# Moving a fused attention and gated-MLP kernel's loads into one GpSimd queue, with cast on load and single-head transposes

## The chip, the cores and the metric

The kernel runs on one core of one Trainium2 chip. The metric is the device time of one execution in microseconds (us), as the median over several executions. A profile is a trace of one execution; its span is 1 to 2 us shorter than the device time. Engines are written as the profile writes them: PE is TensorE, PEld its weight loads, DVE VectorE, ACT ScalarE, POOL GpSimd, SP SyncE (here it only issues DMAs). A queue is the list of transfers that one engine issues, in its order; the core's 16 DMA engines move the data. A packet is one piece of a transfer as the trace records it. PSUM is the memory that the matmuls here write to.

## The reference, cut to what matters

Four batches; 8 heads of 64; 768 positions. A query sees 4 sink positions and a window of 128. The attention output x, 768 x 512 per batch, goes through a gated MLP whose gate mixes positions.

```python
scores = scale * np.matmul(q, k.transpose(0, 1, 3, 2))
keep = (pos[None, :] < n_sink) | in_window          # 4 sinks, window of 128
a = softmax(np.where(keep, scores, -1e9))
x = np.matmul(a, v)                                 # [4, 768, 8*64]
h = gelu(x @ w_in);  u, v = h[..., :512], h[..., 512:]
v_n = layernorm(v) * g_ln
v_s = np.einsum('ts,bsd->btd', w_sg, v_n) + b_sg
out = x + (u * v_s) @ w_out
```

## The kernel before

Both kernels are one list of steps, `STEPS`, that fixes the order of instructions on each engine. A step is a helper's name with batch and pair (or half): `LQ.3.0` loads q of batch 3, `TQ` and `EQ` turn it on TensorE and copy it out of PSUM, `AV` and `NR` make x, `MV` is the v half of the first projection, `RS` the LayerNorm's reciprocal root, `SP`, `GT`, `GM` the gate, `OU`, `RA`, `ST` the output projection, residual and store. Steps of neighbouring batches are interleaved.

All q, k and v loads went in one queue, SP's, in float32, and GpSimd cast each:

```python
def LQ(b, p):
    return nc.sync.dma_start(out=q32.new((b, p)), in_=q[b, 2 * p:2 * p + 2].rearrange("h (p t) d -> p h (t d)", p=128))
def LV(b, p):
    return nc.sync.dma_start(out=v32.new((b, p)).rearrange("p h t d -> p (h t) d"),
                             in_=v[b, 2 * p:2 * p + 2].rearrange("h (t p) d -> p (h t) d", p=128))
def CQ(b, p):     # CK, CV alike
    return cast(q16.new((b, p)).rearrange("p t h d -> p h t d"), ...)      # nc.gpsimd.tensor_scalar
```

For batches 1 to 3, x is turned by two DMA transposes, `XD`, issued on SP's queue too:

```python
def XD(b, half):
    ts = slice(3 * half, 3 * half + 3)
    return nc.sync.dma_start_transpose(out=xT.get(b)[:, ts, :, :].rearrange("p t c i -> p (t c) i"),
                                       in_=x_sb[b][:, ts, :].rearrange("p t d -> p (t d)"))
```

And their place in the order (cut to the loads, transposes and stores of that time): before, all of these are in one queue, so loads that stand behind a transpose cannot pass it.

```
... LQ.3.0 ... LK.3.0 ... XD.1.1 ... XD.1.0 ... ST.0.0 ... ST.0.2 ... LV.3.0 ... LQ.3.1 ... LK.3.1 ... ST.0.1 LV.3.1 ... LQ.3.2 ...
```

The softmax here doesn't subtract the row's maximum and nothing guards it: scores larger than these inputs give would overflow.

## Time and profile before

| | before |
|---|---|
| device time, median | 173.03 us (172.1 to 174.0, 4 runs) |
| span of the profile | 171.1 us |
| PE, DVE, ACT, POOL busy | 88%, 81%, 60%, 56% |
| first matmul of the first projection (MV of batch 0) | 33.5 us |
| DMA transposes, issue to landing | 3.7 to 5.0 us |

The page of the kernel before: busy share of each engine in tenths, in 40 equal slices of the span (4.28 us each), and the DMA queues (packets, MB, share of the time of 16 DMA engines).

```profile
PE   0447889699989899979999999999999999999970
...
DMA  5999989999999999989999200970100374210044
...
q1 hardware_dynamic: 47072, 27.93, 61.5%
q0 software_dynamic: 2368, 2.75, 9.8%
```

PE is nearly full from slice 19 on (counted from 1; 77 us); the losses are at the start. The DMA engines are nearly full up to slice 22. q1 is the queue that SP and ACT issue on; q0 is GpSimd's, which carried only the weights.

### The profile page before, as it was taken

What the parts mean: (1) busy time and instruction counts of PE and PEld (TensorE: products, weight loads), DVE (VectorE), ACT (ScalarE), POOL (GpSimd) and SP (SyncE); (2) the same over time, 40 slices, a digit from 0 to 9 for tenths busy, and PEclk for the clock granted to TensorE, in tenths of its full rate; (3) what the DMA queues carried; (4) which work ended last, traced back from release to release, by engine and by line L of the source; (5) the groups of instructions that cost most, each with busy time, mean ns of one, the idle gap of its engine ahead of it and who ended that gap; (6) DMA issues with size and microseconds to landing.
All of it is one profiled execution on the core that took longest, in us unless ns stands there. A gap on an engine that the chain in (4) does not pass through costs nothing.

```text
span 171.1 us, 3623 instructions
## 1 busy us (share of the span) xinstructions
PE 151.1 (88%) x1388; PEld 90.3 (53%) x1388; DVE 138.7 (81%) x290; ACT 101.9 (60%) x119; POOL 95.9 (56%) x158
## 2 busy tenths in 40 slices
PE   0447889699989899979999999999999999999970
PEld 0323568364655466645576565544565744556530
DVE  6198696629989999999999799848889994959962
ACT  0416887674995768956649985864997006860000
POOL 7789766013899999999599678043306400520000
PEclk9999999999999999999999999999999999999999
DMA  5999989999999999989999200970100374210044
GB/s 166 325 314 240 210 117 195 221 252 246 316 299 297 279 288 298 314 160 214 321 323 281 64 4 17 230 248 0 61 4 0 64 170 180 80 61 0 34 156 184
DMA packets 49617, 30.94 MB, mean 181 GB/s; under 512 B 35904, under 2 KB 46400, under 8 KB 49600
## 3 DMA queue, kind: packets, MB, share of 16 engines
q1 hardware_dynamic: 47072, 27.93, 61.5%
q0 software_dynamic: 2368, 2.75, 9.8%
q8 instruction: 11, 0.18, 0.4%
q10 hardware_dynamic: 160, 0.03, 0.1%
q14 instruction: 6, 0.05, 0.1%
HBM read 24.81 MB, written 6.29 MB: 182 GB/s over the span
## 4 chain that ended last, share of the span: by engine, by line
PE 63%; DVE 20%; ACT 5%; DMA 5%; POOL 3%; issue 2%; DVEq 0%; ACTq 0%
PE mm L466 15%; PE mm L483 11%; PE sc L446 10%; PE sc L399 10%; PE sc L310 5%; PE mm L266 4%; ACT P L318 3%; DVE qT L276 3%; DVE gtmp L471 3%; PE mm L350 3%; DVE x_sb L370 3%; DMA q<-in_q_dram 3%; DVE P L325 3%; DVE wsg_gated L476 2%; PE mm L356 2%
## 5 line engine op out<-in xcount | busy, mean ns | idle before, releaser
L318 ACT ACTIVATE P<-sc 128x1024 bf16<-128x1024 f32 (+1 forms) x48 | 43.7, 953 | 12.2 <-PE sc L310 10.6
L466 PE MATMUL mm<-wsgT,z 128*128 128x384 bf16 x192 | 34.0, 326 | 0.0
L329 POOL TENSOR_SCALAR_AFFINE_SELECT P<-P 128x512 bf16<-128x512 bf16 x28 | 20.1, 719 | 18.2 <-ACT P L318 13.8
L466 PEld LDWEIGHTS <-z 128*128 128x128 bf16 x192 | 18.0, 98 | 12.1 <-issue 1.2
L483 PE MATMUL mm<-w_out_sb,wsg_gated 128*128 128x512 bf16 x96 | 23.0, 379 | 1.1 <-DVE wsg_gated L476 1.1
L399 PE MATMUL sc<-w_in_sb,xT 128*128 128x512 bf16 x96 | 22.4, 379 | 0.2 <-ACT xT L384 0.2
L446 PE MATMUL sc<-xT,w_in_sb 128*128 128x384 bf16 x128 | 22.4, 326 | 0.0
L471 DVE SCALAR_TENSOR_TENSOR gtmp<-mm,g_sb,b_bc 128x384 bf16<-128x384 f32 x32 | 19.3, 611 | 3.6 <-PE mm L466 3.5
L487 DVE TENSOR_TENSOR ot<-mm,x_sb 128x512 f32<-128x512 f32 x24 | 16.1, 683 | 5.4 <-PE mm L483 5.3
L310 PE MATMUL sc<-qT,kT 64*128 64x256 bf16 x192 | 17.0, 287 | 3.8 <-DVE qT L276 1.7
L350 PE MATMUL mm<-v_sb,P 128*128 128x65 bf16 x192 | 18.0, 201 | 1.6 <-DVE P L325 1.4
L404 ACT ACTIVATE vt<-sc 128x1024 f32<-128x1024 f32 x12 | 12.3, 1024 | 11.7 <-PE sc L399 11.7
L182 POOL TENSOR_SCALAR q<-q 128x768 bf16<-128x768 f32 x16 | 14.3, 891 | 8.6 <-DMA q<-in_q_dram 8.6
L370 DVE TENSOR_TENSOR x_sb<-mm,rcp 128x384 bf16<-128x384 f32 x32 | 17.8, 557 | 1.1
L350 PEld LDWEIGHTS <-P 128*128 128x128 bf16 x192 | 15.2, 102 | 5.9 <-issue 2.1
L411 DVE BATCH_NORM_STATS2 st<-vt 128x6 f32<-128x512 f32 x24 | 16.2, 675 | 2.5 <-ACT vt L404 2.5
L325 DVE TENSOR_TENSOR P<-P,mask 128x1024 bf16<-128x1024 bf16 x20 | 16.4, 830 | 1.3 <-ACT P L318 1.1
L356 PE MATMUL mm<-v_sb,P 128*128 128x65 bf16 x160 | 16.9, 200 | 0.0
L446 PEld LDWEIGHTS <-w_in_sb 128*128 128x128 bf16 x128 | 12.4, 98 | 8.4
L281 ACT COPY kT<-mm 128x768 bf16<-128x768 bf16 x16 | 12.8, 801 | 5.6 <-PE mm L266 5.6
L182 POOL TENSOR_SCALAR v_sb<-v 128x768 bf16<-128x768 f32 x16 | 14.9, 937 | 1.9 <-DMA v<-in_v_dram 1.9
L418 POOL TENSOR_SCALAR rs<-mv 128x2 f32<-128x2 f32 x12 | 3.0, 251 | 22.6 <-DVE mv L412 22.2
(61 smaller groups left out, 253.8 us busy)
## 6 DMA issues: line engine op xcount, KB each, us to landing
q<-in_q_dram SPq DMA_DIRECT2D x16, 384.0 KB, 6.6
k<-in_k_dram SPq DMA_DIRECT2D x16, 384.0 KB, 5.8
v<-in_v_dram SPq DMA_DIRECT2D x16, 384.0 KB, 6.9
out_dram<-ot SPq DMA_DIRECT2D x24, 256.0 KB, 2.0
wsg_gated<-in_moe_w_sg_dram POOLq DMA_DIRECT2D x1, 1152.0 KB, 8.8
w_in_sb<-in_moe_w_in_dram POOLq DMA_DIRECT2D x2, 512.0 KB, 7.2
w_out_sb<-in_moe_w_out_dram POOLq DMA_DIRECT2D x1, 512.0 KB, 8.1
b_bc<-in_moe_b_sg_dram SPq DMA_DIRECT2D x1, 384.0 KB
```

What stands on the lines that cost most here:

```text
L182: return nc.gpsimd.tensor_scalar(out=dst, in0=src, scalar1=1.0, scalar2=1.0, op0=ALU.mult, op1=ALU.mult)
L310: nc.tensor.matmul(sc[:, hl, 256 * jl:256 * jl + n], kT[b, p][rows, 128 * j:128 * (j + 1)], qT[b, p][rows, 128 * j:128 * j + n], start=Tru ...
L318: nc.scalar.activation(out=pt[:, :, 0:w], in_=sc_ring[b, p, g][:, :, 0:w], func=AF.Exp, scale=scale)
L325: nc.vector.tensor_mul(pt[:, :, 0:w], pt[:, :, 0:w], m.unsqueeze(1).to_broadcast([128, 2, w]))
L350: nc.tensor.matmul(av[:, il, hl, :], P[b, p, i // 2][:, hl, 256 * (i % 2):256 * (i % 2) + 128], vb[:, h, i, :], start=first, stop=False)
L356: nc.tensor.matmul(av[:, il, hl, :], P[b, p, j // 2][:, hl, 256 * (j % 2) + 128:256 * (j % 2) + 256], vb[:, h, j, :], start=False, stop=False)
L370: nc.vector.tensor_mul(xs[:, 3 * half:3 * half + 3, 128 * p:128 * (p + 1)].rearrange("p t (h d) -> p t h d", h=2), av[:, :, :, 0:Dh], rcp. ...
L399: nc.tensor.matmul(hp[:, jl, :], xT[b][:, j, c, :], w_in_sb[:, c, d_half:2 * d_half], start=(c == 0), stop=(c == KD - 1))
L446: nc.tensor.matmul(hp[:, hf, 0:NH], w_in_sb[:, c, 128 * dc:128 * (dc + 1)], xT[b][:, 3 * hf:3 * hf + 3, c, :], start=(c == 0), stop=(c == ...
L466: nc.tensor.matmul(ps[:, 0:NH], z[b][:, si, 128 * dc:128 * (dc + 1)], wsgT[:, si, NH * hf:NH * (hf + 1)], start=(si == 0), stop=(si == NT ...
L471: nc.vector.scalar_tensor_tensor(out=gtmp.new((b, hf, dc)), in0=mm_ring["g", b, hf, dc][:, 0:NH], scalar=g_sb[:, dc:dc + 1], in1=b_bc[:, N ...
L483: nc.tensor.matmul(ps, gatedT[:, (2 * b + hf) % 3, dc, 128 * tl:128 * (tl + 1)], w_out_sb[:, dc, :], start=(dc == 0), stop=(dc == KU - 1))
```

## The change

The intent: free GpSimd of 42 of its 48 casts by letting the DMA cast q and k, for which they go to GpSimd's queue, and giving most of v's casts to DVE and ACT; keep all loads in one queue in the order in which they are needed, and use the freed time for masks and gating products that DVE did. q and k now lie head by head, so each 128 x 64 block of one head is turned alone, two heads side by side on the two column halves of the array. The sink scores of four head pairs also go side by side. The order of steps is new throughout. The diff, cut to its core (the new `STEPS`, the new places of masks, fills, LayerNorm scalars and gating products are left out):

```diff
-    def LQ(b, p):
-        return nc.sync.dma_start(out=q32.new((b, p)), in_=q[b, 2 * p:2 * p + 2].rearrange("h (p t) d -> p h (t d)", p=128))
+    def load(ring, src, b, i):
+        n = 2 if b == 0 else 4
+        hs = slice(n * i, n * i + n)
+        dst = ring.get((b, n * i // 4))[:, n * i % 4:n * i % 4 + n].rearrange("p h t d -> p h (t d)")
+        return nc.gpsimd.dma_start(out=dst, in_=src[b, hs].rearrange("h (p t) d -> p h (t d)", p=128))
...
     def LV(b, p):
-        return nc.sync.dma_start(out=v32.new((b, p)).rearrange("p h t d -> p (h t) d"),
-                                 in_=v[b, 2 * p:2 * p + 2].rearrange("h (t p) d -> p (h t) d", p=128))
+        return rows(nc.sync if b in DT else nc.gpsimd, v32, v, b, p)      # DT is empty
...
         for t in range(NT):
-            nc.tensor.transpose(ps[:, t, :], src[:, t, :], iden)
+            for hl in range(2):
+                nc.tensor.transpose(ps[64 * hl:64 * hl + 64, t, :], src[:, 2 * (p % 2) + hl, t, :], iden)
...
-        for n, p in enumerate(prs):
-            nc.tensor.matmul(ps, ks_sink[b % 2][:, 128 * p:128 * (p + 1)], qT[b, p][:, 256:768],
-                             start=(n == 0), stop=(n == len(prs) - 1))
+        for p in range(HP):
+            c0 = (128 + ks_w) * p
+            nc.tensor.matmul(ps[ks_w * p:ks_w * (p + 1), :], ks[:, c0:c0 + ks_w], qT[b, p][:, 256:768],
+                             start=True, stop=True)
```

In the new order batch 3's loads stand beside batch 1's transposes (again cut to the loads, transposes and stores). They are in different queues now:

```
... LQ.3.0 ... XD.1.0 ... LK.3.0 ... LV.3.0 ... LV.3.1 ... ST.0.1 ... XD.1.1 ... LQ.3.1 ... LK.3.1 ... LV.3.2 ... ST.0.3 MV.1.0 ... LV.3.3
```

## The prediction

> **What bounds the kernel now.** TensorE, behind a slow start. The page gives PE 88% busy, DVE 81%, ACT 60%, POOL 56%. "Busy" contains matmul latency, so I counted starts in the trace: back to back, a 512-column matmul follows after 216 ns, 384 columns after 162, a 128-column transpose after 56, 65 columns after 29, and two 64-row matmuls start 3 ns apart. At these cadences the PE streams about 135 us of 171. Of the 36 lost, about 23 lie before 35 us (first MV at 34.5 us in the chain of work that ended last), 4 to 5 in the tail, most of the rest at 45 to 75 us, where that chain runs through POOL (LayerNorm queued with casts, 41.2 to 47.6 us) and then DVE (50 to 74 us). From 80 to 160 us the PE streams 97% of the time.
>
> **What the change removes, adds, moves** (mean durations from the instruction groups)
> - POOL: 42 casts of 0.9 us go (-38), 7 affine-select pairs (-9), small LayerNorm operations (-5). It gains 34 load issues, 0.8 to 0.9 us each by the present weight loads (+31, more if 1,536-row v loads cost more), and 17 gating products (estimate 0.9 us, +16). Still near 90 us, but loads, masks and gating now wait behind each other.
> - DVE: 17 gating products (0.48 us) and 3 PSUM copies (0.95) go, -11; seven casts, seven masks, LayerNorm scalars and two xT copies come, about +11.
> - ACT: +4.
> - PE: sink scores of batches 1 to 3 go from four 216 ns matmuls to four side by side: -2 us. Transposes: 192 become 384 of half width. If two run together as the 64-row matmuls do, nothing changes; if their weight loads serialise, up to 0.3 us for each of 32 tiles, +10. The Trainium skill (TensorEngine Tiling, Restrictions) says column tiling excludes fast weight load; no trace here shows it yet. I take +3.
> - DMA: cast loads need the GpSimd queue (Trainium skill, DMA: Bandwidth & Descriptors, "SWDGE vs HWDGE vs iDMA"; the four weight loads agree). In the DMA records a packet of that queue costs about 13 ns more than one of the SP queue (98 against 85 ns at 2 KB, 22 against 9 at 4 B). So v rows go from 18 to about 31 ns, a v load from 1.8 to 3 us of all 16 engines. Total about 128 us: fits, but one ordered queue delivers batch 1's second q, k about 55 us, close to need.
>
> **On the critical path.** First scores (10.6 us now, held by DVE waiting for the sink v until 8.6 us) come 1 us earlier; first MV perhaps 2 to 3 earlier. LayerNorm/DVE stretch: -4 to -5. Sink scores -2, transposes +3, late batch-1 loads and port contention +1 to +2. Sum about -5.
>
> **Predicted: 168 us, 160 to 177 in 8 of 10. Faster by over 2%: 0.60; within 2%: 0.27; slower: 0.13.**
>
> **What would show it.** Right: first scores before 10 us; the GpSimd queue carrying nearly all load packets, 256 B ones near 31 ns; transposes in pairs a few ns apart, 12 in 0.35 to 0.45 us; no POOL cast of q or k after batch 0; PE idle of 45 to 75 us halved. Wrong: transposes at 50 ns each (+8); v issues above 1.5 us on POOL; PE waiting on DMA for batch 1's q or k; DVE waiting on POOL for gating.
>
> **What would make it wrong.** 256 B packets far above 31 ns; serial half-width weight loads; POOL blocked by a load whose buffer is not free, delaying masks.

## More of the kernel before

The instructions that read or write xT, the turned x, in the kernel before: count, duration in ns as least, median and most, first and last start; then who waited for it. The last line is from issue to landing.

```profile
L388 SPq DMA_TRANSPOSE xT<-x_sb x6: 1426/1452/1906, 71.5 to 137.6; - x6
...
DMA to landing us min/median/max: 3.7/4.3/5.0
```

SP's queue in the kernel before around batch 1's two transposes (start, duration of the issue in us, line, transfer). They stand at 71.46 and 76.28 us, and what follows them in the queue (the v loads from 79.23 on) starts after them.

```profile
71.46 1.91 SPq L388 DMA_TRANSPOSE xT<-x_sb  x1
74.72 0.34 SPq L490 DMA_DIRECT2D out_dram<-ot  x1
76.28 1.45 SPq L388 DMA_TRANSPOSE xT<-x_sb  x1
77.82 1.30 SPq L490 DMA_DIRECT2D out_dram<-ot  x2
79.23 0.39 SPq L178 DMA_DIRECT2D v<-in_v_dram  x1
```

## The result, and the profile after

The changed kernel took 184.19 us (183.81 to 185.47, 4 runs) against 173.03. The ratio of the two is 1.066, with a 95% interval of 1.058 to 1.074. (Every ratio here is the mean time of one kernel's fast runs over that of the other's of the same rounds, so it is not quite the ratio of the medians.) It is slower, and outside the predicted range of 160 to 177.

The same rows of the page after. A slice is now 4.6 us.

```profile
PE   0567948999799999459049999999999999999990
...
PEclk9996596999999999978858999999999999999999
DMA  5999999999995139999971000099000048111044
...
q0 software_dynamic: 12128, 14.94, 44.5%
q1 hardware_dynamic: 14240, 9.87, 21.0%
```

The hole is in slices 17 to 21 (73.5 to 96.5 us): PE reads 4, 5, 9, 0, 4 tenths, while the DMA row reads 9 there (7 in the last slice), so the engines that move data were busy while TensorE stood still. The granted clock drops in and after the hole: from 75 to 100 us PE was busy 13.0 of 25 us and its granted clock was 0.80 (in e1 below, without the hole, 23.8 us and 1.00). The chain of work that ended last, around the hole (start, duration, what):

```profile
71.53 0.54 PE sc L344 x8
72.07 1.06 PE mm L505 x5
73.14 21.32 DMA xT<-x_sb
94.46 0.05 issue
94.51 4.24 PE sc L428 x12
```

The chain hangs for 21.32 us on one transfer, batch 1's second transpose. The instructions on xT, and the longest waits of the kernel after on DMAs (engine, line, what it waited for: us in total, times, longest):

```profile
L419 SPq DMA_TRANSPOSE xT<-x_sb x6: 1323/1441/7436, 68.5 to 150.3; - x6
...
DMA to landing us min/median/max: 3.6/4.3/11.6
```

```profile
DVE ot L509 <- DMA out_dram<-ot: 13.4, 2, 7.4
PEld L428 <- DMA xT<-x_sb: 12.9, 2, 7.8
PE sc L428 <- DMA xT<-x_sb: 11.9, 2, 7.3
```

The median landing is as before, 4.3 us; one of six, batch 1's first, took 11.6, and by the chain the second took 21.3. (The line of landings covers only the transposes that the tool could match.) The stores of batch 0 on the same queue came late too. SP's queue at that time, and GpSimd's loads beside it (a line with x4 runs from the first issue to the end of the last, waits between them included):

```profile
68.47 2.08 SPq L419 DMA_TRANSPOSE xT<-x_sb  x1
72.41 0.34 SPq L512 DMA_DIRECT2D out_dram<-ot  x1
73.14 7.44 SPq L419 DMA_TRANSPOSE xT<-x_sb  x1
80.67 15.40 SPq L512 DMA_DIRECT2D out_dram<-ot  x4
```

```profile
67.92 0.80 POOL L182 DMA_DIRECT2D q<-in_q_dram  x1
68.71 0.90 POOL L182 DMA_DIRECT2D k<-in_k_dram  x1
69.60 1.04 POOL L185 DMA_DIRECT2D v<-in_v_dram  x1
...
71.81 1.07 POOL L185 DMA_DIRECT2D v<-in_v_dram  x1
```

Seven of batch 3's eight loads were issued from 67.9 to 75 us (the eighth at 76.8), on the other queue, in the same 10 us as the two transposes. They were not needed so soon: in the kernel before, all but two of batch 3's twelve (smaller) loads came after the transposes in the queue, from 79.23 us on.

What the DMA engines did then can be counted in the trace's DMA records: packets started in each 2 us, by queue and size. A transpose is 1,536 packets of 256 B; q and k travel as 768 B (the size written), v on GpSimd's queue as 4,096 B.

```
after            GpSimd 768 B   GpSimd 4096 B   SP 256 B (transposes)
72 to 74 us               151               0                     707
74 to 76 us               224               0                     695
82 to 84 us               258              11                     265
84 to 86 us               370               0                     384
86 to 88 us               275              34                     322
88 to 90 us                18              71                     104
90 to 92 us                 0              67                     143

the same transposes with the loads held back (experiment e1)
72 to 74 us               166               0                    1347
74 to 76 us                 0               0                    1270
```

From 82 to 88 us, where both queues had work throughout, the engines served about one packet of each in turn, with three times the bytes written for the loads; against v's 4,096 B the transposes got one to two packets per large one, and only 104 and 143 in 2 us. The first transpose, from 72 to 76 us, got three to five packets for each one of 768 B; why the shares differed there stays open. In e1, nearly alone, each transpose's 1,536 packets were through in 1.9 us, about 800 per us. The Trainium skill states such turns ("DMA: Bandwidth & Descriptors", section "Queues, rings and completion order"): each DMA engine goes round robin between the queues it has work for, packet by packet. The trace agrees with one turn each from 82 to 88 us, with 258:265 and 370:384, but not from 72 to 76 us, with 151:707 and 224:695.

The packets also divide the 21.32 us. For the first 5.3 us (73.1 to 78.5) the second transpose had no packet under way: in SP's own queue the first transpose (packets from 72.3 to 77.9 us) and a store (76.9 to 81.5) stood in front of it, both slowed. Its own packets then took 15.4 us, to 93.8; in e1 they took 1.9.

Before, the v loads that follow the transposes stood behind them in the same queue, and could not take turns with them.

### The profile page after: what moved, and what is told of

The parts are those of the page before. It is cut to its first block, busy times and chain, and to the rows that moved or that the text cites. A ratio compares the mean times of both kernels' runs of the same rounds, so it can differ in the third digit from the quotient of the medians.

```text
span 183.8 us, 3933 instructions
## 1 busy us (share of the span) xinstructions
PE 151.8 (83%) x1567; PEld 90.3 (49%) x1580; DVE 138.1 (75%) x307; ACT 105.3 (57%) x125; POOL 89.1 (48%) x121
## 2 busy tenths in 40 slices
DMA packets 26386, 25.06 MB, mean 136 GB/s; under 512 B 11136, under 2 KB 21632, under 8 KB 26368
## 3 DMA queue, kind: packets, MB, share of 16 engines
q0 software_dynamic: 12128, 14.94, 44.5%
## 4 chain that ended last, share of the span: by engine, by line
PE 68%; DMA 15%; DVE 7%; ACT 4%; issue 2%; SPq 1%; POOL 1%; DVEq 0%
PE mm L488 18%; DMA xT<-x_sb 12%; PE sc L468 11%; PE sc L428 10%; PE mm L505 10%; PE sc L344 6%; PE mm L294 4%; PE mm L384 4%; ACT P L352 3%; DMA vs<-in_v_dram 3%; PE mm L390 2%; PE mm L394 2%; DVE P L359 2%; DVE x_sb L404 1%; DVE v_sink L283 1%
## 5 line engine op out<-in xcount | busy, mean ns | idle before, releaser
L428 PE MATMUL sc<-w_in_sb,xT 128*128 128x512 bf16 x94 | 25.2, 419 | 12.2 <-DMA xT<-x_sb 11.9
L509 DVE TENSOR_TENSOR ot<-mm,x_sb 128x512 f32<-128x512 f32 x24 | 16.1, 686 | 19.8 <-DMA out_dram<-ot 13.4
L498 POOL TENSOR_TENSOR wsg_gated<-gtmp,uT 128x384 bf16<-128x384 bf16 x17 | 16.8, 991 | 18.7 <-DVE gtmp L493 18.4
L449 POOL TENSOR_TENSOR rs<-rs,neg_half 128x4 f32<-128x4 f32 (+1 forms) x8 | 6.9, 865 | 33.6 <-DVE rs L444 31.5
L505 PE MATMUL mm<-w_out_sb,wsg_gated 128*128 128x512 bf16 x87 | 22.3, 379 | 0.7 <-issue 0.3
L428 PEld LDWEIGHTS <-xT 128*128 128x128 bf16 x96 | 9.8, 106 | 25.4 <-DMA xT<-x_sb 12.9
L363 POOL TENSOR_SCALAR_AFFINE_SELECT P<-P 128x512 bf16<-128x512 bf16 x21 | 14.5, 689 | 15.6 <-ACT P L352 15.6
L359 DVE TENSOR_TENSOR P<-P,mask 128x1024 bf16<-128x1024 bf16 (+1 forms) x27 | 21.5, 816 | 0.0
L185 POOL DMA_DIRECT2D v<-in_v_dram x16 | 16.9, 1058 | 8.9 <-DMA wsg_gated<-in_moe_w_sg_dram 3.8
## 6 DMA issues: line engine op xcount, KB each, us to landing
k<-in_k_dram POOLq DMA_DIRECT2D x6, 384.0 KB, 15.4
```

The source lines that it names most:

```text
L185: return eng.dma_start(out=ring.new((b, p)).rearrange("p h t d -> p (h t) d"), in_=src[b, 2 * p:2 * p + 2].rearrange("h (t p) d -> p (h t) ...
L359: nc.vector.tensor_mul(pt[:, :, 0:w], pt[:, :, 0:w], m.unsqueeze(1).to_broadcast([128, 2, w]))
L428: nc.tensor.matmul(hp[:, jl, :], xT[b][:, j, c, :], w_in_sb[:, c, d_half:2 * d_half], start=(c == 0), stop=(c == KD - 1))
L505: nc.tensor.matmul(ps, gatedT[:, (2 * b + hf) % 3, dc, 128 * tl:128 * (tl + 1)], w_out_sb[:, dc, :], start=(dc == 0), stop=(dc == KU - 1))
```

## The experiments

All experiments edit the changed kernel's steps or one helper. Each was timed beside the kernel before on the same chip. The theory (A in the expectations) is that batch 3's loads on GpSimd's queue starve batch 1's transposes on SP's queue. Rivals: B, that the loads cost by themselves and not through the transposes (by their place in GpSimd's order of instructions, or v's loads by their issue and descriptors), or that dearer work on PE and DVE does; C, that the transpose stands behind a late store in SP's own queue.

### e1: hold batch 3's loads until the transposes have landed

```diff
-EX.1.3.2 TK.2.2 LQ.3.0 GT.0.1.2 XD.1.0 ... LK.3.0 ... LV.3.0 ... LV.3.1 ... XD.1.1 ... LQ.3.1 ... LK.3.1 ... LV.3.2 ... LV.3.3
+EX.1.3.2 TK.2.2 LQ.3.0 GT.0.1.2 XD.1.0 ... XD.1.1 ... MK.2.1.1.P LK.3.0 LV.3.0 LV.3.1 LQ.3.1 LK.3.1 LV.3.2 LV.3.3
-HOLDS = "LG<LWS"
+HOLDS = "LG<LWS LK.3.0<XD.1.1"
```

> The changed kernel with one move: the seven loads of batch 3 behind its first q load are issued after the masks that now follow them, and wait until batch 1's second DMA transpose has landed. Theory A (the DMA transposes of batch 1, made of 256 B packets on the SP queue, share each DMA engine turn by turn with the long packets of the GpSimd queue's loads): both transposes land within 5 us of issue, the 11.9 us of PE waiting for xT and most of the 13.4 us of DVE waiting for the output stores go, time 166 to 171 us. Theory B (the loads' place in the GpSimd instruction queue, or dearer PE and DVE work all over, makes the kernel slow): at most 4 us better, 180 to 184 us.

Measured: correct, 172.03 us (170.6 to 172.72), ratio to the kernel before 0.994 (0.987 to 1.002). The edit of seven loads' place gives back 12 us of 184.2. The transposes now land like this, and PE's wait for them and DVE's for the stores are gone from the list of waits:

```profile
L419 SPq DMA_TRANSPOSE xT<-x_sb x6: 1322/1440/1584, 68.6 to 136.6; - x6
...
DMA to landing us min/median/max: 3.7/4.3/6.3
```

That is theory A's main claim; and as PE and DVE have the same work as in the changed kernel, dearer work there is not the loss. Batch 1's first transpose took the 6.3 us, over the 5 that I expected (why is not shown); the second took 3.9, by its semaphore. And the time is 1 us over the range that I expected. The chain of e1 (start, duration, what) shows a new wait that the hold itself made:

```profile
77.71 0.80 POOL k L182
78.51 7.46 DMA v<-in_v_dram
85.97 0.08 issue
86.06 0.83 POOL v_sb L210
86.89 1.03 POOL rs L449
```

GpSimd waits until 85.97 us for a v load of batch 3 that is now late, to cast it, and only then computes `rs`, the LayerNorm of batch 1, for which DVE and TensorE wait. Experiment e5 follows this up.

### e2: turn batch 1's x on TensorE, loads where the change put them

```diff
-... XD.1.0 ... XD.1.1 ...
+... XT.1.0 XE.1.0.A XT.1.1 XE.1.1.D XT.1.2 XE.1.2.A XT.1.3 XE.1.3.D ...
```

> The changed kernel with batch 1's x turned by 24 TensorE transposes and four PSUM copies (two ACT, two DVE) instead of the two DMA transposes; the loads stay where they are. Theory A: the wait goes as well, since no small packets are on the critical path; PE pays about 1.4 us and the output stores still stand against the loads, so 167 to 173 us. Theory B: 181 to 186 us.

Measured: 171.38 us (170.54 to 171.84), ratio 0.990 (0.983 to 0.997), but the result was wrong (relative error 0.17): by my reading of the order, my insertion needed more PSUM slots than the ring of four has, so two steps read slots that had been overwritten. The time is as theory A expects, yet I did not lean on it; e7 is the same idea in an order that is right.

### e3: the store of batch 0 behind the transpose

```diff
-QK.2.0.1 ST.0.1 OU.0.5 EX.2.0.0 MK.2.0.2.D XD.1.1 KS.2.0
+QK.2.0.1 OU.0.5 EX.2.0.0 MK.2.0.2.D XD.1.1 ST.0.1 KS.2.0
```

> The changed kernel with the output store that stands between the two DMA transposes of batch 1 moved behind the second. Theory A (turns between the two queues): the second transpose still needs 10 us or more from issue to landing, because its packets still alternate with the loads' packets; time 179 to 184 us. Rival C (the second transpose only queues behind that store on the SP queue): it lands within 6 us and the time falls to about 170 us.

Measured: correct, 187.41 us (one run, its state unknown), above the ranges of both. Rival C falls: nothing is gained by taking the store from in front of the transpose. The second transpose still landed 19.2 us after its issue, and its packets alone ran from 77.4 to 91.4 us. The chain shows the store in the transpose's place:

```profile
75.19 3.55 SPq L419
78.79 13.69 DMA out_dram<-ot
```

The store now stood behind the second transpose in SP's queue. Its own 128 packets ran only from 89.5 to 91.4 us, so most of its 13.7 us is waiting behind the transpose.

### e4: all v loads back on SP's queue

```diff
     def LV(b, p):
-        return rows(nc.sync if b in DT else nc.gpsimd, v32, v, b, p)
+        return rows(nc.sync, v32, v, b, p)
```

> The changed kernel with all v loads back on the SP queue, q and k still cast on the GpSimd queue. Theory A: the GpSimd queue keeps only 768 B packets of about 80 ns, so the transposes of batch 1 suffer less from turns, but they now stand in one queue behind batch 3's v rows: 174 to 182 us. Theory B (v on the GpSimd queue, its issue time and descriptors, is what costs): about 170 us.

Measured: correct, 197.74 us (196.28 to 198.52), ratio 1.143 (1.135 to 1.151). Rival B's form about v falls: the v loads are not better off outside GpSimd's queue. It is also worse than theory A's own range, because I had not thought of the start, where it does the same damage. On SP's queue v travels as 256 B packets (49,426 packets in all against 26,386), and these take turns with the weights' larger ones on GpSimd's queue: in two neighbouring stretches of 2 us around 20 us, 298 and 302 packets of 1,024 B against 299 and 307 of 256 B; later 223 and 225 of 1,536 B against 227 and 224. One to one at both sizes there. The eight v loads of the first two batches kept SP issuing for 45 us (44.5 us by the sum of the eight issues):

```profile
5.05 45.22 SPq L185 DMA_DIRECT2D v<-in_v_dram  x8
```

and three engines waited for them in turn (waits of e4):

```profile
POOL v_sb L210 <- DMA v<-in_v_dram: 18.7, 2, 11.3
PE mm L384 <- DVE P L359: 15.1, 1, 15.1
DVE v_sb L209 <- DMA v<-in_v_dram: 13.8, 1, 13.8
```

This is the change's mechanism at its clearest: while large packets ran on one queue, small ones on the other got about one turn in two and a fraction of the bytes.

### e5: e1, and the two casts of late v moved behind the LayerNorm on GpSimd

```diff
-NR.2.0.1 BN.1.1 AV.2.1.0 CV.3.0.P GV.1.2 MU.1.3 BN.1.2 RS.1.1 MU.1.2 GU.1.3 CV.3.1.P MU.1.1 NM.1.1 GU.1.2 NR.2.1.0 RS.1.2 Z.1.2.A
+NR.2.0.1 BN.1.1 AV.2.1.0 GV.1.2 MU.1.3 BN.1.2 RS.1.1 MU.1.2 GU.1.3 MU.1.1 NM.1.1 GU.1.2 NR.2.1.0 RS.1.2 CV.3.0.P CV.3.1.P Z.1.2.A
```

> Edit: e1 (batch 3's loads held until batch 1's second DMA transpose is issued and landed in order), and in addition the two GpSimd copies of batch 3's v that stood ahead of batch 1's LayerNorm sums in GpSimd's order are moved behind them. Theory A2 (what e1 kept losing is GpSimd waiting for the late v of batch 3 ahead of batch 1's LayerNorm): 168 to 170 us, and no GpSimd wait for a v load on the chain between 78 and 90 us. Rival (the rest of e1's loss is in the late second transpose or elsewhere): 171.5 to 172.5 us, as e1.

Measured: correct, 169.78 us (168.98 to 172.3, 5 runs), ratio of the fast runs 0.980 (0.976 to 0.984). Two of the five runs, the profiled one among them, were over 1.5% above the fastest and count as slow; the three fast ones are 168.98, 169.69 and 169.78. With e1 at 172.03 that is about 2.3 us, on different chips but each against the same kernel before (0.994 and 0.980). It fits theory A2. Since the profile fell into a slow run, I do not compare its times with the others'; its chain between 78 and 92 us no longer holds a v load, but a k load.

### e6: e5, and the sink's v out of DVE's way at the start

```diff
-EQ.0.1.A TK.0.0 EQ.0.0.D LV.0.1 EK.0.0.A TK.0.1 VSM.0 ... VSM.1 ... VSM.3 ... VSM.2 ...
+(VSM.0 behind MK.0.1.0, the other three ahead of WE.3)
```

In the changed kernel the chain of the first 12 us (start, duration, what) was the load of the sink's v (5.42 us, landing at 9.83) and DVE's products with it, which stood ahead of the first keys:

```profile
4.41 5.42 DMA vs<-in_v_dram
9.95 0.69 DVE v_sink L283
10.65 0.07 DVE ks_sink L317
```

> Edit: e5, and the multiplication of the attention sink's v, which stands first on VectorE and waits for the sink's v load, moved behind the first keys' work. Theory (the late sink v delays the first keys on VectorE at the start): the first matmul of the first projection 1 to 2 us earlier than in e5, and 167 to 169 us in all. Rival (the start is set by the loads of the first pairs, not by that wait): within 0.5 us of e5.

Measured: correct, 168.82 us (168.32 to 172.41, 4 runs, one slow), ratio 0.976 (0.973 to 0.980). The first projection begins at 29.6 us in place of 31.8 in the changed kernel and 32.0 in e1 (e5's profile is of a slow run). Against e5's fast runs (mean 169.5) its fast runs (mean 168.65) gain 0.8 us, little more than the 0.5 us that the rival allows; e11 below is e6 again and came out at 169.6, so this last step is not settled by the times, only by the profile's start. As a whole, e6 beats both kernels. Its PE row has no hole:

```profile
PE   0494759899969999999998999999999999999980
```

### e7: batch 1's x turned on TensorE, correctly, with the moves of e5 and e6

```diff
-... XD.1.0 ... XD.1.1 ... (batch 3's loads stay nearly where the change put them)
+... RA.0.5 ST.0.5 XT.1.0 RA.0.3 QK.2.1.1 XT.1.1 XE.1.0.A SK.2.0 XE.1.1.D EX.2.1.1 XT.1.2 ST.0.3 SX.2.0 MK.2.1.2.D XT.1.3 XE.1.2.A XE.1.3.D ...
```

> Edit: the changed kernel with its loads where the change put them, but batch 1's x turned by TensorE as the other batches' is (this time in an order that keeps the ring of PSUM slots right), with the two moves of e5 and e6. The result should be correct. Theory A (only the DMA transposes suffered from the competing loads): 166 to 170 us; the stores of batch 0 still land late, without cost. Rival (the competition with loads also hurts the stores or the later loads on the critical path): over 171 us.

Measured: correct, 169.93 us (169.42 to 170.68), ratio 0.984 (0.981 to 0.988). The loads are not held in time, and the loss is gone all the same: take away either side of the contest and the 12 us come back. (e7 has the other two moves as well; e2, without them, was at 171.38 us.) As the loads keep nearly their place in GpSimd's order, rival B's first form falls too. The four transposes that remain all land within 3.8 us:

```profile
L420 SPq DMA_TRANSPOSE xT<-x_sb x4: 1427/1434/1568, 101.8 to 134.8; - x4
...
DMA to landing us min/median/max: 3.7/3.7/3.8
```

The stores were late without cost, as I expected: by their semaphores the four of batch 0 that were issued from 70 to 77 us landed after 4.8 to 7.7 us (in the changed kernel 9.8 to 14.25 us for those from 72 to 84 us, where they also stood behind the transposes), and no wait for a store is in the list of waits.

### e8: the changed kernel with only the move of the sink's v

> Edit: the changed kernel with only the move of the sink's v multiplication. Theory: the start gains 1 to 2 us, but the transposes of batch 1 still starve, so the time is 182 to 185 us, and the wait for the transposes stays over 15 us in sum. Rival (an earlier start brings the transposes out of the way of the loads): under 180 us.

The edit is that of e6 alone. Measured: correct, 183.99 us (one run). The chain has `71.40 20.12 DMA xT<-x_sb`, 1.2 us shorter than in the changed kernel, and the time is the changed kernel's median within 0.2 us. So this move alone does not undo the loss. What became of the earlier start is not shown: in the two profiles the second transpose lands 2.9 us earlier (91.5 to 94.5 us), the span is 1.5 us shorter (182.3 to 183.8), and e8 is one run of unknown state. (The sum of PE's waits for them was 9.6 us and not over 15; the rest of the gap is put down to other names in the list of waits.)

### e9, e10, e11: what the side-by-side parts are worth, on e6

e9 issues the six transposes of one head, then the six of the other. e10 puts the sink scores back to four full-width matmuls that accumulate. e11 is e6 unchanged.

```diff
 e9:
-        for t in range(NT):
-            for hl in range(2):
+        for hl in range(2):
+            for t in range(NT):
 e10:
-            nc.tensor.matmul(ps[ks_w * p:ks_w * (p + 1), :], ks[:, c0:c0 + ks_w], qT[b, p][:, 256:768],
-                             start=True, stop=True)
+            nc.tensor.matmul(ps, ks[:, 128 * p:128 * (p + 1)], qT[b, p][:, 256:768],
+                             start=(p == 0), stop=(p == HP - 1))
```

> Edit on e6: the two heads' transposes of one row block are no longer issued next to each other; six of the one head go first, then six of the other, so that pairs cannot overlap (but at the seam). Theory (the transposes side by side are what keeps the half-width form cheap): twelve starts some 50 ns apart take about 0.6 us in place of 0.4, +0.2 us for each of 32 tiles, 6 us of TensorE's time; since TensorE is nearly full from 80 us on, the time rises by 3 to 6 us over e6 of the same call. Rival (the pairs do not matter, TensorE has room or half-width transposes follow each other as closely anyway): within 1 us of e6.

> Edit on e6: the sink scores of batches 1 to 3 as four full-width matmuls that accumulate, as in the kernel before, in place of four side by side. Theory (TensorE's time in the full part counts): 0.97 us in place of 0.33 for each of three batches, so 1.5 to 2 us over e6 of the same call. Rival (it is hidden): within 0.7 us of e6.

> e6 unchanged, once more, as the measure for the two others on the same chip, and to see with more rounds whether it is over 2% faster than the kernel before: ratio 0.974 to 0.980.

Measured, all correct, same chip and same rounds: e9 170.13 us (169.53 to 171.17), ratio to the kernel before 0.984 (0.980 to 0.989); e10 170.34 us (169.82 to 170.71), ratio 0.984 (0.980 to 0.988); e11 169.82 us (168.31 to 171.19, one run slow), ratio 0.979 (0.974 to 0.985).

e9 did not do what its theory needed. Its transposes still overlapped: starts 30 and 26 ns apart in alternation, in place of 3 and 53, so the first and the last of twelve start 389 ns apart (median) in place of 306. TensorE seems to let the second head's six begin on the free column half while the first head's are under way (an inference from the starts; the records do not name the half). The sum over all tiles is 2.5 us of TensorE's time (13.4 against 10.9), and the fast runs' means differ by 0.7 us (170.3 to 169.6), within the intervals. So e9 bounds nothing about serial transposes.

e10 did: the matmuls start 216 ns apart in place of 3 to 4, which is 0.64 us more for each of three batches, or 1.9 us. The time rose by 0.75 us (170.34 to 169.59, means of fast runs), inside the intervals: under half of the saved PE time is seen. I expected 1.5 to 2; it falls nearer the rival.

All experiments in one table (fast runs against the kernel before; us are medians):

| kernel | us | ratio | what it tells |
|---|---|---|---|
| changed kernel | 184.19 | 1.066 | |
| e1 batch 3's loads held | 172.03 | 0.994 | the contention is 12 us |
| e2 x turned on TensorE (wrong result) | 171.38 | 0.990 | time only |
| e3 store behind transpose | 187.41 | (one run) | not SP's own order |
| e4 v on SP's queue | 197.74 | 1.143 | v's small packets on SP's queue lose too |
| e5 = e1 + late v casts moved | 169.78 | 0.980 | the hold's own cost |
| e6 = e5 + sink's v moved | 168.82 | 0.976 | the best version |
| e7 = turned on TensorE + both moves | 169.93 | 0.984 | the other side of the contest taken away |
| e8 sink's v moved alone | 183.99 | (one run) | this move alone does not undo the loss |
| e9, e10, e11 on e6 | 170.13, 170.34, 169.82 | 0.984, 0.984, 0.979 | side-by-side parts: about 0.7 us each, inside the intervals |

## Why the prediction was wrong, point by point

The step that failed is the term "late batch-1 loads and port contention +1 to +2". It was mis-sized and misplaced: the contention cost 12 us, which e1 gives back by moving seven loads. The argument behind it was a sum over the whole kernel ("Total about 128 us: fits"), and a look at whether q and k of batch 1 come in time (they did: PE's wait for q was 7.4 us, of which 6.9 at the very start). What the sum cannot see is who shares the engines at the moment when a short transfer is on the critical path. The change moved the loads out of SP's queue, and with that removed an order that nobody had written down: before, later loads waited behind the transposes. Of this the prediction says nothing; the transposes, which the diff does not touch, were not in it.

The rest of the sum, term by term:

- **First scores before 10 us**: 9.9 us. Right. **First MV 2 to 3 us earlier**: 31.8 against 33.5, 1.7 us; with the sink's v moved (e6) 29.6.
- **GpSimd near 90 us, DVE unchanged**: 89.1 and 138.1 us busy (before 95.9 and 138.7). Right. **v issues below 1.5 us**: 1.06 us on average. Right. **Gating product 0.9 us**: 0.99.
- **Transposes in pairs a few ns apart, 12 in 0.35 to 0.45 us**: starts 3 to 4 ns apart, then 53; 24 take 0.79 us on the chain where 12 full-width ones took 0.67 (`87.74 0.67 PE mm L266 x12` before). That is +0.12 for each of 16 groups of this size, about +2 in place of +3 (by the sums of first to last starts, 11.3 us against 10.9, less still). The Trainium skill ("TensorEngine Tiling (Array Packing)", section "Restrictions") says that column tiling excludes fast weight load; this trace shows no more cost than that.
- **Sink scores side by side**: 0.33 us in place of 0.97. The size was right; e10 shows that little of it reaches the end.
- **v rows at 31 ns**: wrong. On GpSimd's queue 16 rows of 256 B share one packet of 4,096 B, which takes 202 ns (median): 12.6 ns per row. The error was on the pessimistic side. The load's own time did not hurt; but beside these large packets the transposes got their fewest turns.
- **PE idle of 45 to 75 us halved**: not seen as such; PE was busy 28.1 us of 30 before and 28.5 after.
- **Sum about -5**: with the contention out (e1) the gain is about 1 us, and with the casts moved too that then waited for held loads in front of the LayerNorm (e5) about 3 us (169.78 against 172.79). e6's -4.0 contains the move of the sink's v (about 0.8, not settled), which the change did not have. So over half of the predicted gain was there under the contention; the rest is not shown.

What stays open: how the 1 us or so of e9 and e10 splits, and whether e6 is over 2% faster. Its ratios are 0.976 and 0.979, but the second interval reaches 0.985.

## What to carry to other kernels

When loads move from one DMA queue to another, ask what they used to wait behind: one queue is an order, two queues are a race that is settled packet by packet. Before a short transfer that the critical path waits for (a transpose, a store that frees a buffer), hold bulk loads of the other queue that are not needed yet, and size the danger by packets, not by bytes or by the sum of DMA time. And when a load is held, look at which in-order engine consumes it and what stands behind that consumer.

## What the Trainium skill lacked or had wrong

- "DMA: Bandwidth & Descriptors", "Rules for kernel authors", says that spreading DMAs over the issuing engines does not help and only saves issue time. It lacks that it can hurt: a transpose on SP's queue beside loads on GpSimd's landed after 11.6 and 21.3 us in place of 4.3 (median), and 12 us of 184 went there.
- The same page, "Queues, rings and completion order", has the round robin by packets, and the runs agree (258:265 and 370:384 packets in 2 us; in e4 223:227 at 1,536 B against 256 B). It lacks the consequence, that the side with small packets gets a small share of bytes, and that turns are not always one to one: against 4,096 B packets the transposes got 104 to 89 and 143 to 67, and the first of them 707 to 151 and 695 to 224 against 768 B.
- The same page, "SWDGE vs HWDGE vs iDMA", gives a packet's preferred limit of 4,096 B. It lacks that the two queues cut the same load differently: v rows of 256 B went 16 to a packet on GpSimd's queue (12.6 ns per row), and one to a packet on SP's (49,426 packets in e4, 26,386 in the changed kernel).
- The same page, "Issuing engines are not separate DMA queues", calls the time to issue usually small. Under contention it was not: a transpose's issue took 7.44 us (before 1.45), and one v load's on SP in e4 up to 11.2 us.
- "TensorEngine Tiling (Array Packing)", "Restrictions", does not say what pairs of half-width transposes cost without fast weight load. Here twelve of them started within 306 ns (median, e11), against 5 steps of 56 ns for six full-width ones. Its "Key Properties" says that tiles work independently; e9's starts (30 and 26 ns apart) suggest this also for matmuls that are not next to each other in the program, but the records do not name the half, so it is not shown.
